# Half a pass less in the first layers, and one chunk of the second MLP ahead of the last chunk of the first

## The chip, the cores and the metric

One core of one Trainium2 chip. The metric is the device time of one execution in microseconds (us). The engines are named as the profile names them: PE (TensorE) with PEld for its weight loads, DVE (VectorE), ACT (ScalarE), POOL (GpSimd), and SP (SyncE), whose queue issues every DMA of this kernel.

## The reference

An RWKV-like recurrence over 768 steps, then two MLPs, each over 3072 tokens of width 320 with a hidden width of 2048:

```python
y_t = r_t @ state                                   # 4 x 8 heads, head_dim 40
state = state * w_t - (state @ a_t) b_t^T + v_t k_t^T
x = y as [3072 tokens, 320]
h = x @ w_in;  x = (h * cos(h)) @ w_out             # first MLP
h = x @ w_in2; out = (s * relu(h)**2 + b) @ w_out2  # second MLP
```

The four weight matrices arrive as 64-bit floats.

## The kernel before

The sequence is cut into 12 chunks c of 64 steps; with 4 batches a chunk is 256 tokens. For each chunk there is a preparation (`prep`: decays, inverse of a triangular matrix), a serial recurrence (`chain`, twice, for the two halves pg of the heads), and the first MLP on the chunk (`mlp` with `m1_f` and `m1_s`). After all of that stands the second MLP, again by 12 chunks j (`m2_f`, `m2_s`). Everything is emitted through `Recorder`, a planner: it collects the instructions of one block (`do` makes a block), gives each a duration and a priority (its longest path to the end, raised by `base`), and writes out an order for each engine by simulating the engines. `schedule(until=...)` does this in three calls: until the preparation's memory is free, until the recurrence's memory is free, to the end. Each engine then works strictly in that order, SP too, so a DMA that waits holds up all DMAs behind it.

Precision: a float32 operand is split in two float16 halves, high and low, and a product takes the passes high x high, high x low and low x high. In `first` a hidden block of 128 columns (ff, 16 of them) takes 8 matmuls of 256 token columns into one PSUM tile `hp`: the 320 input rows stand as 3 heads of 40 on 120 partitions, three groups, of which the last one has only two heads, so that its three products fit in two passes once the low weights have been copied below the high ones (tile `wlo`, two DMAs for each pair of blocks in `w_in_pair`). Two blocks ff = 2p and 2p + 1 share one `hp`; as soon as both are done ACT and DVE (in the first MLP also POOL) make the activation and split it in `gh` and `gl`, and two steps later `m1_s` or `m2_s` does the second layer, 6 matmuls of 320 columns for each half m of the tokens and each p. At most 2 `hp` and 2 `op` (results of the second layer) live at a time; all PSUM tiles come from 8 buffers.

Weights: a raw 64-bit chunk is loaded (`w_in_load`, `w_out_load`), DVE turns it into float32 with three instructions (`float32`), ACT makes the high half, POOL scales in place and makes the low half. For the first MLP raw chunks lie in the memory of the finished weights as far as `place` allows, the others in buffers of tag `xs`. The second MLP's output weights `v2` are loaded when the preparation's memory is free, its input weights `w2` only when the recurrence's memory is free. The recurrence's result goes to DRAM (`xs`, the DMA x<-yhl) and comes back as the MLP's operand (`x1_load`, the DMA xs<-x); the first MLP's result goes through DRAM too (`x2`, the DMA x2f<-x).

All recorded instructions carry line 407, the planner's `emit`, so tiles tell them apart. In the profile w and v stand for both MLPs' weights (numbers are left out of names), wraw and vraw for raw chunks in buffers, XX for the decays, rhp, uhp, ytp, tsp and the like for the recurrence's PSUM tiles.

Of the kernel before, what the change touches and what calls it, by code (L numbers as in the profile page):

```python
# [25 lines left out]
C = 64  # L26
# [3 lines left out]
HEADS = [0, 3, 6, 1, 4, 7, 2, 5]  # L30
# [416 lines left out]
class Fast:  # L447
# [73 lines left out]
    def norm(self, rows, sq, i, k=0):  # L521

        nc = self.nc
        ps = self.pp.tile([128, 2], F32, tag="at", bufs=8, name="np")
        for j, x in enumerate(sq):
            nc.tensor.matmul(ps, x, rows[0:x.shape[0]], start=(j == 0), stop=(j == len(sq) - 1))
        nc.vector.tensor_reduce(out=self.norms[:, k, i:i + 1], in_=ps, axis=AX.X, op=ALU.max)
# [11 lines left out]
    @staticmethod  # L539
    def place(dst, k):  # L540

        q = k + 3 if k < 5 else k if k < 8 else k - 2 if k < 10 else None
        if q is not None:
            return dst[:, 2 * q:2 * q + 2].rearrange("p f a n -> p (f a n)").bitcast(U64)

    def w_in_load(self, src, dst, k):
        p, tag, raws, n = self.wtags[:4]
        raw = self.place(dst, k) if n == 128 else None
        if raw is not None:
            raw = raw.rearrange("p (a n) -> p a n", a=3)  # L550
        else:
            raw = p.tile([120, 3, n], U64, tag=tag, bufs=raws, name="wraw")
        self.RAW["i", k] = raw
        self.nc.sync.dma_start(out=raw, in_=src[:, :, k * n:k * n + n])

    def w_out_load(self, src, dst, k):
        p, tag, raws, n = self.wtags[:4]
        raw = self.place(dst, k) if n == 128 else None
        if raw is None:
            raw = p.tile([128, DM], U64, tag=tag, bufs=raws, name="vraw")  # L560
        self.RAW["o", k] = raw
        self.nc.sync.dma_start(out=raw, in_=src[k * 128:k * 128 + 128, :])

    def w_in_pair(self, dst, name, k):

        nc = self.nc
        p, _, _, n, tag, bufs = self.wtags
        lo = p.tile([80, 2, 128], F16, tag=tag, bufs=bufs, name="wlo")
        m = n // 128
        for i in range(0, 2, m):  # L570
            self.w_in_chunk(dst, name, k * 2 // m + i, n, lo[:, i:i + m])
        for j in range(2):
            nc.sync.dma_start(out=dst[80:120, 2 * k:2 * k + 2, 4 + j], in_=lo[j * 40:j * 40 + 40])

    def w_in_chunk(self, dst, name, k, n, lo):
        nc = self.nc
        raw = self.RAW["i", k]
        st = self.float32(raw)
        m = n // 128
        wv = dst[:, k * m:k * m + m].rearrange("p f a n -> p a f n")  # L580
        sv = st.rearrange("p a (f n) -> p a f n", f=m)
        for a, r, x in ((0, 120, sv[:, 0:2]), (4, 80, bc(sv[0:80, 2], 1, [80, 2, m, 128]))):
            nc.scalar.activation(wv[0:r, a:a + 2], x, AF.Copy, scale=SW)
        nc.gpsimd.tensor_scalar(out=st, in0=st, scalar1=SW, scalar2=1.0, op0=ALU.mult, op1=ALU.mult)
        nc.gpsimd.tensor_tensor(out=wv[:, 2:4], in0=sv[:, 0:2], in1=wv[:, 0:2], op=ALU.subtract)
        nc.gpsimd.tensor_tensor(out=lo, in0=sv[0:80, 2], in1=wv[0:80, 4], op=ALU.subtract)

    def w_out_chunk(self, dst, name, k):
        nc = self.nc
        st = self.float32(self.RAW["o", k])  # L590
# [7 lines left out]
    def w_in_test(self, src, name, k):  # L598

        nc = self.nc  # L600
        sq = self.pm.tile([120, 2, 3, 128], BF16, tag="xs", name="wsq", bufs=4)
        for i, (rows, a, n) in enumerate(((120, 0, 2), (80, 4, 1))):
            nc.scalar.activation(sq[0:rows, :, 2 * i:2 * i + n], src[0:rows, 2 * k:2 * k + 2, a:a + n], AF.Square, scale=1.0 / SW,
                                 accum_out=self.st[0:rows, STAT_IX[name], 2 * k + i:2 * k + i + 1])
        if name == "w1":
            for f in range(2):
                self.norm(self.ones, [sq[0:j, f, i] for i, j in enumerate((120, 120, 80))], 2 * k + f, 1)

    def w_out_test(self, src, name, k):
        self.square(src[:, 2 * k:2 * k + 2, 0], name, k, 1.0 / SW)  # L610
# [821 lines left out]
```

## Time and profile before

| | us |
|---|---|
| median of 3 runs | 1165.01 |
| lowest and highest run | 1154.4, 1169.88 |
| time of the profiled execution | 1152.13 |
| its span, first to last instruction | 1150.4 |
| PE busy in the span | 993.0 (86%) |
| DVE, ACT, POOL busy | 706.4, 728.9, 431.4 |
| mean granted TensorE clock, as a share of full | 0.939 |

The span is the time between the first and the last instruction; the time of that execution has 1.7 us more around it. The profiled execution is shorter than all three timed ones. Busy time of PE counts matmuls by their modelled ends, which overlap, so pauses of a tenth of a microsecond between two matmuls don't show as idle; starts of matmuls do show them.

### The profile page before, as it was taken

To read this page: it belongs to the slowest core of one execution; us is meant where nothing else is said; L and a number is where in the kernel's file an instruction comes from. 1 tells how busy PE (TensorE), PEld (TensorE's weight loads), DVE (VectorE), ACT (ScalarE), POOL (GpSimd) and SP (SyncE) were. 2 spreads that over 40 slices of the span, in tenths; PEclk is the share of its full clock that TensorE was granted. 3 is DMA by queue.
4 is the path that set the end of the run, shared out by engine and by line. 5 is a ranking of instruction groups with operands and counts; after the bars stand their busy time and mean duration, and the time that the engine had idled before them with its cause. 6 is when DMAs were issued, how large, how long until landed. Compare 5 with 4: busy or idle time off the path is not lost.

```text
span 1150.4 us, 37826 instructions
## 1 busy us (share of the span) xinstructions
PE 993.0 (86%) x16094; PEld 802.2 (70%) x16094; DVE 706.4 (61%) x1390; ACT 728.9 (63%) x1608; POOL 431.4 (37%) x430
## 2 busy tenths in 40 slices
PE   3026889998899799979999998938999999999997
PEld 3025667877677687768788786826888888888885
DVE  6799797829563648382848363978454455544443
ACT  3345678968788777767879664735565544544443
POOL 2576649445544454555465422547300000000000
PEclk9998669998899699989999998969999999999999
DMA  9763454444433543443444304473100100001000
GB/s 226 210 201 120 120 190 153 136 139 132 158 103 94 177 139 102 141 152 115 145 152 144 106 30 137 135 185 88 30 24 24 24 24 23 24 24 25 24 15 23
DMA packets 74755, 121.15 MB, mean 105 GB/s; under 512 B 16500, under 2 KB 47348, under 8 KB 73556
## 3 DMA queue, kind: packets, MB, share of 16 engines
q1 hardware_dynamic: 74580, 118.67, 34.1%
q8 instruction: 128, 2.10, 0.7%
q14 instruction: 47, 0.39, 0.1%
HBM read 72.71 MB, written 12.29 MB: 74 GB/s over the span
## 4 chain that ended last, share of the span: by engine, by line
PE 66%; DVE 11%; DMA 8%; SPq 6%; ACT 6%; issue 3%; POOL 0%; ACTq 0%; DVEq 0%
PE hp L407 26%; PE op L407 23%; SPq L407 6%; PE rhp L407 3%; PE ytp L407 3%; PE uhp L407 3%; DVE XX L407 2%; DMA XX<-in_w 2%; DVE wraw L407 2%; DVE v L407 2%; PE dtp L407 1%; DMA x2f<-x 1%; DMA xs<-x 1%; DMA wraw<-in_w 1%; PE ydp L407 1%
## 5 line engine op out<-in xcount | busy, mean ns | idle before, releaser
L407 PEld LDWEIGHTS <-w 120*128 120x128 f16 x3072 | 297.2, 99 | 73.4 <-DMA xs<-x 21.6
L407 PE MATMUL op<-v,gh 128*128 128x320 f16 x1536 | 325.0, 302 | 1.7 <-ACT gh L407 1.7
L407 PE MATMUL op<-v,gl 128*128 128x320 f16 x768 | 231.3, 301 | 1.7 <-POOL gl L407 1.7
L407 PE MATMUL hp<-xs,w 120*128 120x256 f16 x1536 | 204.5, 284 | 23.2 <-DMA xs<-x 22.6
L407 PE MATMUL hp<-x2s,w 120*128 120x256 f16 x1536 | 188.8, 272 | 0.0
L407 POOL TENSOR_TENSOR gl<-q,gh 128x512 f16<-128x512 f32 x96 | 116.5, 1221 | 183.2 <-ACT gh L407 175.8
L407 PEld LDWEIGHTS <-gh 128*128 128x128 f16 x1536 | 143.2, 98 | 49.8 <-ACT gh L407 2.1
L407 DVE SCALAR_TENSOR_TENSOR q<-q,s_t 128x512 f32<-128x512 f32 x96 | 72.3, 753 | 120.8 <-ACT q L407 118.5
L407 ACT ACTIVATE q<-hp 128x512 f32<-128x512 f32 x96 | 57.2, 596 | 126.2 <-PE hp L407 125.9
L407 DVE SCALAR_TENSOR_TENSOR q<-hp,q 128x512 f32<-128x512 f32 x96 | 65.4, 684 | 58.9 <-ACT q L407 58.1
L407 PEld LDWEIGHTS <-gl 128*128 128x128 f16 x768 | 75.4, 98 | 33.0 <-POOL gl L407 2.3
L407 DVE SCALAR_TENSOR_TENSOR gl<-q,b_t,gh 128x512 f16<-128x512 f32 x96 | 72.0, 750 | 38.0 <-ACT gh L407 35.6
L407 ACT ACTIVATE gh<-q,b_t 128x512 f16<-128x512 f32 x96 | 69.1, 720 | 32.3 <-DVE q L407 31.2
L407 ACT ACTIVATE q<-hp,half_pi 128x512 f32<-128x512 f32 x96 | 64.7, 682 | 30.5 <-PE hp L407 29.1
L407 POOL TENSOR_TENSOR kb<-kb,XX 128x512 f32<-128x512 f32 x44 | 57.4, 1316 | 69.8 <-DVE XX L407 47.0
L407 DVE TENSOR_TENSOR_SCAN XX<-XX,starts 128x264 f32<-128x264 f32 x96 | 67.0, 752 | 16.5 <-DMA XX<-in_w 14.2
L407 ACT ACTIVATE gh<-q 128x512 f16<-128x512 f32 x96 | 59.4, 625 | 12.8 <-DVE q L407 12.0
L407 PEld LDWEIGHTS <-KB 120*128 120x128 f16 (+1 forms) x704 | 28.3, 101 | 46.9 <-DMA KB<-kbl 31.4
L407 PE MATMUL rhp<-UF,M 64*64 64x40 f32 (+1 forms) x1536 | 54.2, 230 | 1.0 <-ACT UF L407 0.6
L407 ACT ACTIVATE UF<-uhp 32x320 f32<-32x320 f32 x96 | 41.1, 428 | 22.1 <-PE uhp L407 20.3
L407 ACT ACTIVATE R<-rhp 32x320 f32<-32x320 f32 x96 | 41.1, 429 | 21.4 <-PE rhp L407 19.6
L407 POOL TENSOR_TENSOR kbl<-kb,kbh 128x1024 f16<-128x1024 f32 x22 | 46.8, 2129 | 20.3 <-ACT kbh L407 20.2
(178 smaller groups left out, 1739.3 us busy)
## 6 DMA issues: line engine op xcount, KB each, us to landing
XX<-in_w SPq DMA_DIRECT2D x12, 1056.0 KB
kb<-in_kb SPq DMA_DIRECT2D x24, 512.0 KB
ar<-in_ar SPq DMA_DIRECT2D x22, 512.0 KB
KB<-kbh SPq DMA_DIRECT2D x88, 80.0 KB
ars<-arh SPq DMA_DIRECT2D x88, 80.0 KB
v<-in_v SPq DMA_DIRECT2D x20, 320.0 KB
wraw<-in_w SPq DMA_DIRECT2D x8, 720.0 KB
SS<-SHL SPq DMA_DIRECT2D x88, 50.0 KB
```

Source lines behind the costliest of these rows:

```text
L407: f(*a, **k)
```

## The change

The input rows now stand as 128 + 128 + 64 partitions. `first` does 7 matmuls over all partitions for each hidden block: of the last 64 input rows, high weights and low weights stand one above the other on 128 partitions and multiply the high half of the input in one pass. What is left, high weights by the low half of the last 64 input rows, is a matmul of 64 partitions (`tail`). `rows` puts the tails of a step's two blocks on the partitions 0 to 63, those of the next step's on 64 to 127; `tails` (blocks `m1_t`, `m2_t`) emits the tail of block 2p - 1 and that of block 2p next to each other, ahead of the 7 matmuls of block 2p. The tails of blocks 0 and 15 stand alone. So an `hp` tile is finished one step later, the activation is a block of its own (`m1_g`, `m2_g`) behind that, and 3 `hp` may live at a time. The copies of low weights by DMA (`wlo`) are gone, `x1_load` is 4 DMAs instead of 1.

Of the second MLP's weights, 12 of 16 blocks of both matrices now go into the preparation's memory, with raw chunks in place or in the 5 buffers of tag `xs`; the other 4 go into the recurrence's memory. The first 6 steps of the second MLP's chunk 0 are emitted ahead of the first MLP's last chunk, its rest behind it.

```diff
+    def place(dst, k, size):
+        v = dst.rearrange("p f a n -> p (f a n)")
+        n, part = v.shape[1], v.shape[1] // dst.shape[1]
+        ends = [n - i * size * 4 for i in range(n // (size * 4))]
+        last = dict.fromkeys(ends, -9)
+        for i in range(k + 1):
+            l = [(last[e], e) for e in ends if (e - size * 4) // part > i]
+            q = min(l, default=(i, None))
+            if q[0] >= i - 1:
+                q = (i, None)
+            else:
+                last[q[1]] = i
+        e = q[1]
+        return None if e is None else v[:, e - size * 4:e].bitcast(U64)
...
+    @staticmethod
+    def rows(ff):
+        return ff // 2 % 2 * 64
...
-        for a, r, x in ((0, 120, sv[:, 0:2]), (4, 80, bc(sv[0:80, 2], 1, [80, 2, m, 128]))):
-            nc.scalar.activation(wv[0:r, a:a + 2], x, AF.Copy, scale=SW)
+        nc.scalar.activation(wv[:, 0:3], sv, AF.Copy, scale=SW)
         nc.gpsimd.tensor_scalar(out=st, in0=st, scalar1=SW, scalar2=1.0, op0=ALU.mult, op1=ALU.mult)
-        nc.gpsimd.tensor_tensor(out=wv[:, 2:4], in0=sv[:, 0:2], in1=wv[:, 0:2], op=ALU.subtract)
-        nc.gpsimd.tensor_tensor(out=lo, in0=sv[0:80, 2], in1=wv[0:80, 4], op=ALU.subtract)
+        nc.gpsimd.tensor_tensor(out=wv[:, 3:5], in0=sv[:, 0:2], in1=wv[:, 0:2], op=ALU.subtract)
+        r = slice(64 - self.rows(k * m), 128 - self.rows(k * m))
+        nc.gpsimd.tensor_tensor(out=wv[r, 2], in0=sv[r, 2], in1=wv[r, 2], op=ALU.subtract)
...
+    def second(self, wd, vd, ff0):
+        self.ff0 = ff0
+        for k in range(wd.shape[1]):
+            self.do(self.w_in_load, self.i["w2"], wd, k)
+            self.do(self.w_in_chunk, wd, "w2", k)
+            self.do(self.w_out_load, self.i["v2"], vd, k)
+            self.do(self.w_out_chunk, vd, "v2", k)
...
-        x = self.XS[c] = self.pm.tile([120, 2, 6, 128], F16, tag="xs", name="xs", bufs=4)
-        self.nc.sync.dma_start(out=x, in_=self.x0[c].rearrange("f j p n -> (j p) f n"))
-    def first(self, ps, w, x, ff):
-        for i, (a, b) in enumerate(((0, 0), (0, 1), (1, 2), (1, 3), (2, 0), (3, 2), (4, 4), (5, 5))):
-            self.nc.tensor.matmul(ps, w[:, ff, a], x[:, b // 2, b % 2], start=(ff % 2 == 0 and i == 0), stop=True,
-                                  skip_group_check=True)
+        x = self.XS[c] = self.pm.tile([128, 2, 3, 2, 128], F16, tag="xs", name="xs", bufs=5)
+        v, x = self.x0[c].rearrange("f h e n -> f (h e) n"), x.rearrange("p f i k t -> p f i (k t)")
+        for f in range(2):
+            self.nc.sync.dma_start(out=x[:, f, 0:2], in_=v[f, 0:256].rearrange("(i p) n -> p i n", i=2))
+        for h in range(2):
+            self.nc.sync.dma_start(out=x[h * 64:h * 64 + 64, :, 2], in_=v[:, 256:320].rearrange("f p n -> p f n"))
+    def tail(self, ps, w, x, ff):
+        r = slice(self.rows(ff), self.rows(ff) + 64)
+        self.nc.tensor.matmul(ps[:, ff % 2], w[ff][r, 2], x[r, 2, 1], start=(ff % 2 == 0), stop=True, skip_group_check=True)
+    def tails(self, p, w, x):
+        hp = self.HP
+        hp[p] = self.ph.tile([128, 2, TB], F32, tag="at", bufs=8, name="hp")
+        if p:
+            self.tail(hp[p - 1], w, x, 2 * p - 1)
+        self.tail(hp[p], w, x, 2 * p)
+    def first(self, p, k, w, x):
+        ff, hp = 2 * p + k, self.HP
+        for a, i, b in ((0, 0, 0), (0, 0, 1), (1, 1, 0), (1, 1, 1), (2, 2, 0), (3, 0, 0), (4, 1, 0)):
+            self.nc.tensor.matmul(hp[p][:, k], w[ff][:, a], x[:, i, b], start=False, stop=True, skip_group_check=True)
+        if ff == NFF - 1:
+            self.tail(hp[p], w, x, ff)
...
     def m1_f(self, c, p, k):
-        nc = self.nc
-        if k == 0:
-            self.HP[p] = self.ph.tile([128, 2, TB], F32, tag="at", bufs=8, name="hp")
-        ps, x = self.HP[p], self.XS[c]
-        ff = 2 * p + k
-        self.first(ps[:, k, :], self.w1, x.rearrange("p f (i k) t -> p i k f t", k=2), ff)
-        if k == 0:
-            return
+        x = self.XS[c]
+        self.first(p, k, self.W1, x.rearrange("p f i k t -> p i k f t"))
+    def m1_g(self, c, p):
+        nc, ps = self.nc, self.HP[p]
...
-    def mlp(self, f, s, j):
+    def mlp(self, t, f, g, s, j, lo=0, hi=NFF // 2 + 2):
         lag = 2
-        for p in range(NFF // 2 + lag):
+        for p in range(lo, hi):
             for k in range(2):
                 if p < NFF // 2:
+                    if k == 0:
+                        self.do(t, j, p)
                     self.do(f, j, p, k)
+                if k == 0 and 1 <= p <= NFF // 2:
+                    self.do(g, j, p - 1)
                 if p >= lag:
                     self.do(s, j, p - lag, k)
...
-            rec = self.nc = Recorder(nc, {"any": {"at", "xs", "q"}, "cls": {"XT": 3, "rhp": 3, "hp": 2, "op": 2, "xs": 2, "M2": 2, "q": 4, "att": 6}})
+            rec = self.nc = Recorder(nc, {"any": {"at", "xs", "q"}, "cls": {"XT": 3, "rhp": 3, "hp": 3, "op": 2, "xs": 2, "M2": 2, "q": 4, "att": 6}})
...
-                self.mlp(self.m1_f, self.m1_s, c)
+                if c < NC - 1:
+                    self.mlp(*m1, c)
+                else:
+                    self.nc.base[self.nc.blk] = 26
...
-            self.v2 = pv.tile([128, NFF, 2, DM], F16, name="v2")
-            self.wtags = pv, "vraw", 4, 128, None, 0
-            for k in range(NFF):
-                self.do(self.w_out_load, self.i["v2"], self.v2, k)
-                self.do(self.w_out_chunk, self.v2, "v2", k)
+            n = 12
+            v2 = pv.tile([128, n, 2, DM], F16, name="v2")
+            w2 = pv.tile([128, n, 5, 128], F16, name="w2")
+            self.second(w2, v2, 0)
+            self.W2, self.V2 = ([t[:, f] for f in range(n)] for t in (w2, v2))
+            self.do(self.x2, 0)
+            self.mlp(*m2, 0, 0, n // 2)
+            half = dict(self.HP), dict(self.GH)
+            self.mlp(*m1, NC - 1)
+            self.HP, self.GH = half
             rec.schedule(until=("attn",))
             es_a.close()
             es_b = ExitStack()
             self.pb = pool(es_b, "late")
-            self.w2 = self.pb.tile([120, NFF, 6, 128], F16, name="w2")
-            self.wtags = self.pb, "braw", 6, 256, "blo", 5
-            for k in range(FF // 256):
-                self.do(self.w_in_load, self.i["w2"], self.w2, k)
-                self.do(self.w_in_pair, self.w2, "w2", k)
+            v2b = self.pb.tile([128, NFF - n, 2, DM], F16, name="v2b")
+            w2b = self.pb.tile([128, NFF - n, 5, 128], F16, name="w2b")
+            self.wtags = self.pb, "braw", 8, 128
+            self.second(w2b, v2b, n)
+            self.W2 += [w2b[:, f] for f in range(NFF - n)]
+            self.V2 += [v2b[:, f] for f in range(NFF - n)]
             for j in range(NC):
-                self.do(self.x2, j)
-                self.mlp(self.m2_f, self.m2_s, j)
+                if j:
+                    self.do(self.x2, j)
+                self.mlp(*m2, j, 0 if j else n // 2)
```

## Rows read from the trace of the kernel before

**Rows 1.** The page, parts 1 and 2: busy time, and 40 equal slices.

```profile
PE 993.0 (86%) x16094; PEld 802.2 (70%) x16094; DVE 706.4 (61%) x1390; ACT 728.9 (63%) x1608; POOL 431.4 (37%) x430
...
PE   3026889998899799979999998938999999999997
```

**Rows 2.** Windows: stretch, length; PE, PEld, DVE, ACT, POOL busy; clock; DMA share, GB/s.

```profile
150.00:752.00 602.00, 563.28 (x11694) 453.73 (x11689) 379.13 (x867) 461.24 (x1028) 298.75 (x239) 0.94 0.40 130
752.00:771.00 19.00, 0.16 (x2) 0.00 (x0) 11.17 (x20) 5.06 (x12) 7.25 (x8) 0.62 0.83 203
771.00:805.00 34.00, 28.54 (x213) 21.95 (x214) 29.23 (x30) 18.15 (x35) 26.78 (x22) 0.86 0.44 111
805.00:1141.00 336.00, 336.00 (x2846) 272.23 (x2844) 160.53 (x235) 171.03 (x355) 9.10 (x32) 1.00 0.09 23
```

**Rows 3.** Timeline of PE at 771: start, length, instruction, idle before and releaser.

```profile
771.26 1.03 PE L407 MATMUL hp<-xs,w 120*128 120x256 f16 x4 [19.10 <-DMA xs<-x]
```

**Rows 4.** Timeline of SP, 749 to 762.

```profile
749.95 0.69 SPq L407 DMA_DIRECT2D x<-yhl  x2
754.02 3.63 SPq L407 DMA_DIRECT2D wraw<-in_w  x4
757.69 0.60 SPq L407 DMA_DIRECT2D xs<-x  x1
758.34 3.11 SPq L407 DMA_DIRECT2D wraw<-in_w  x2
```

**Rows 5.** The chain of waits in the second MLP: start, length, piece.

```profile
856.58 2.62 PE hp L407 x24
...
884.30 2.62 PE hp L407 x24
```

**Rows 6.** Timeline of PE around 656, from whole-array matmuls to 40-row transposes.

```profile
655.73 0.30 PE L407 MATMUL op<-v,gh 128*128 128x320 f16 x1
655.86 0.30 PE L407 MATMUL op<-v,gl 128*128 128x320 f16 x1
656.09 0.29 PE L407 MATMUL tsp<-ident,SHL 40*80 40x40 f16 x6
```

**Rows 7.** Timeline of PE, the last of these transposes and what follows it.

```profile
656.38 0.19 PE L407 MATMUL tsp<-ident,SHL 40*80 40x40 f16 x1
656.51 0.31 PE L407 MATMUL op<-v,gh 128*128 128x320 f16 x1
```

**Rows 8.** Timeline of PE at 103.4: two matmuls of 40 rows on different array halves.

```profile
103.40 0.28 PE L407 MATMUL s2p<-ars,XT 40*128 40x64 f32 x2
```

**Rows 9.** Groups by line and form: busy, mean ns of one, idle before, releaser.

```profile
L407 PE MATMUL hp<-xs,w 120*128 120x256 f16 x1536 | 204.5, 284 | 23.2 <-DMA xs<-x 22.6 <-issue 0.5 <-ACT SD L407 0.2
...
L407 DVE SCALAR_TENSOR_TENSOR q<-q,s_t 128x512 f32<-128x512 f32 x96 | 72.3, 753 | 120.8 <-ACT q L407 118.5
L407 DVE SCALAR_TENSOR_TENSOR gl<-q,b_t,gh 128x512 f16<-128x512 f32 x96 | 72.0, 750 | 38.0 <-ACT gh L407 35.6
L407 ACT ACTIVATE gh<-q,b_t 128x512 f16<-128x512 f32 x96 | 69.1, 720 | 32.3 <-DVE q L407 31.2
...
L407 ACT ACTIVATE q<-hp 128x512 f32<-128x512 f32 x96 | 57.2, 596 | 126.2 <-PE hp L407 125.9
```

**Rows 10.** Windows from the release of the preparation's memory on.

```profile
695.00:725.00 30.00, 25.56 (x489) 20.01 (x478) 11.99 (x29) 16.36 (x38) 4.63 (x6) 0.83 0.61 197
725.00:757.00 32.00, 26.71 (x351) 20.75 (x348) 28.84 (x52) 21.78 (x47) 19.13 (x22) 0.99 0.25 75
```

**Rows 11.** Groups by line and form: DVE's conversion of raw chunks.

```profile
L407 DVE SCALAR_TENSOR_TENSOR v<-v 128x320 int32<-128x320 int32 x40 | 31.9, 803 | 0.1
...
L407 DVE SCALAR_TENSOR_TENSOR w<-w 120x384 int32<-120x384 int32 x20 | 18.0, 917 | 0.1
...
L407 DVE TENSOR_SCALAR v<-v 128x320 int32<-128x320 int32 x20 | 10.0, 502 | 11.1 <-DMA v<-in_v 6.5 <-PE np L407 4.6
...
L407 DVE TENSOR_SCALAR w<-w 120x384 int32<-120x384 int32 x10 | 7.2, 718 | 1.0 <-DMA w<-in_w 1.0
```

More of the change, by code (lines that the diff above doesn't have):

```diff
@@ L519, in square, with norm @@
         self.nc.scalar.activation(j, x, AF.Square, scale=scale, accum_out=self.st[rows, STAT_IX[name], i:i + 1])
-    def norm(self, rows, sq, i, k=0):
+    def norm(self, sq, i, k=0):
         nc = self.nc
         ps = self.pp.tile([128, 2], F32, tag="at", bufs=8, name="np")
-        for j, x in enumerate(sq):
-            nc.tensor.matmul(ps, x, rows[0:x.shape[0]], start=(j == 0), stop=(j == len(sq) - 1))
+        for j, (x, rows) in enumerate(sq):
+            nc.tensor.matmul(ps, x, rows, start=(j == 0), stop=(j == len(sq) - 1))
         nc.vector.tensor_reduce(out=self.norms[:, k, i:i + 1], in_=ps, axis=AX.X, op=ALU.max)
@@ L551, in w_in_load @@
         else:
-            raw = p.tile([120, 3, n], U64, tag=tag, bufs=raws, name="wraw")
-        self.RAW["i", k] = raw
-        self.nc.sync.dma_start(out=raw, in_=src[:, :, k * n:k * n + n])
+            raw = p.tile([128, 3, n], U64, tag=tag, bufs=raws, name="wraw")
+        self.RAW["i", dst.tensor.name, k] = raw
+        self.nc.sync.dma_start(out=raw, in_=src[:, :, self.ff0 * 128 + k * n:self.ff0 * 128 + k * n + n])
     def w_out_load(self, src, dst, k):
-        p, tag, raws, n = self.wtags[:4]
@@ L558, in w_out_load @@
-        raw = self.place(dst, k) if n == 128 else None
+        p, tag, raws, n = self.wtags
+        raw = self.place(dst, k, DM) if p is self.pm else None
         if raw is None:
             raw = p.tile([128, DM], U64, tag=tag, bufs=raws, name="vraw")
-        self.RAW["o", k] = raw
-        self.nc.sync.dma_start(out=raw, in_=src[k * 128:k * 128 + 128, :])
-    def w_in_pair(self, dst, name, k):
-        nc = self.nc
[L567 to L573, printed above, removed]
@@ L1006, in yt @@
                              accum_out=self.st[:, STAT_IX["y"], 2 * c + pg:2 * c + pg + 1])
-        self.norm(self.halves, [sq[:, h] for h in range(4)], 2 * c + pg)
+        self.norm([(sq[:, h], self.halves) for h in range(4)], 2 * c + pg)
     def xs(self, c):
@@ new lines, in x2 @@
+        nc.sync.dma_start(out=xt[:, :, 320:384], in_=v[:, :, 256:320])
+        q = self.pm.tile([128, 2, 2, 384], F16, tag="xs", name="x2q", bufs=5)
+        xs = self.XS[NC + j] = self.pm.tile([128, 3, 2, 2, 128], F16, tag="xs", name="x2s", bufs=5)
+        for m in range(2):
+            nc.scalar.activation(q[:, 0, m], xt[:, m], AF.Copy, scale=SX2)
+            nc.vector.scalar_tensor_tensor(out=q[:, 1, m], in0=xt[:, m], scalar=SX2, in1=q[:, 0, m], op0=ALU.mult, op1=ALU.subtract)
+            ps = self.pp.tile([128, 3, 2, 128], F16, tag="at", bufs=8, name="xtp")
+            for i in range(3):
+                for b in range(2):
+                    nc.tensor.transpose(ps[:, i, b], q[:, b, m, i * 128:i * 128 + 128], self.ident)
+            nc.vector.tensor_copy(xs[:, :, :, m], ps)
@@ L1090, in m2_f, with m2_t, m2_g @@
+    def m2_t(self, j, p):
+        x = self.XS[NC + j]
+        self.tails(p, self.W2, x.rearrange("p i b m t -> p i b (m t)"))
+    def m2_f(self, j, p, k):
+        x = self.XS[NC + j]
+        self.first(p, k, self.W2, x.rearrange("p i b m t -> p i b (m t)"))
+    def m2_g(self, j, p):
+        nc, ps = self.nc, self.HP[p]
         q = self.pm.tile([128, 2, TB], F32, tag="q", name="q", bufs=8)
@@ L1233, in run @@
             rec.vector.tensor_copy(self.YT[:, :, 16:32], bc(self.up[:, 0:16], 1, [128, 16, 16]))
-            self.wtags = self.pm, "xs", 4, 128, "wlo", 2
+            self.wtags = self.pm, "xs", 5, 128
+            self.ff0 = 0
+            self.W1, self.V1 = ([t[:, f] for f in range(NFF)] for t in (self.w1, self.v1))
+            m1 = self.m1_t, self.m1_f, self.m1_g, self.m1_s
+            m2 = self.m2_t, self.m2_f, self.m2_g, self.m2_s
             self.prep(0)
```

118 lines of the change are left out of this document (52 added, 66 removed).

## The prediction

> **What bounds the kernel now.** I read the page first: PE is busy in 86% of the span, and its slices show three stages with one hole, the slice that reads 3 between the eights and nines [rows 1]. Then one table of windows cut at those places [rows 2]. From 150 to 752 (recurrence and first MLP) PE is busy 563 of 602 us at a granted clock of 0.94, which is mostly the 2.4 GHz level: almost full, so work taken from or given to PE there counts for most of its price, not all. From 752 to 771 PE stands still. From 771 to 805 it does the last chunk of the first MLP, partly at 1.2 GHz (mean 0.86). From 805 to 1141 it is busy 336 of 336 us at 1.00: the second MLP is bound by PE alone, and what a pass costs there is paid in full. What ends the 19.1 us of idleness is the DMA xs<-x, the operand of the last chunk [rows 3]; SP's timeline says why it is late: four raw weight chunks of 0.72 MB were issued ahead of it as soon as the recurrence's memory was free, and it lands 13.6 us after its issue at 757.69 [rows 4].
>
> **The first layers.** In the second MLP 24 first-layer matmuls stand in the chain with 2.62 us, 109 ns each, and the same piece comes back after 884.30 - 856.58 = 27.72 us, one chunk [rows 5]. Before, a step's two blocks take 16 passes; now 14, and two tails of half the rows. If two tails cost one pass, a chunk saves 7 passes (7 pairs; the tails of blocks 0 and 15 stand alone and save none), 0.76 us. Whether they do is what this prediction hangs on, and the trace has the parts.
>
> *Do two halves of the array work at once?* Yes: two matmuls of 40 rows by 128 columns, on row halves 0 and 64, take 0.28 us together where one takes 0.27: they start 7 ns apart [rows 8].
>
> *What does it cost to get there and back?* The kernel already goes from whole-array matmuls to the half-row kind: the second layer's matmuls start 0.13 us apart (320 columns), but the transposes of 40 rows start 0.23 us after the last of them, 0.093 us late in the unrounded starts [rows 6]. Back again: the last transpose (40 columns, 0.017 us at 109 ns for 256) starts at 656.38, the next whole-array matmul at 656.51, 0.122 us later in the unrounded starts, so 0.10 us late [rows 7]. Some 20 other entries and exits of the same transposes gave the same two figures. Neither pause shows as idle time, since matmuls' modelled ends cover it.
>
> So a pair costs 0.093 + 0.007 + 0.109 + 0.10 = 0.309 us in place of two passes, 0.218: 0.091 us more. A lone tail costs 0.093 + 0.109 + 0.10 = 0.302 in place of 0.109: 0.193 more. A chunk: 7 x 0.091 + 2 x 0.193 = 1.02 us **more**. Bounds: without pauses -0.71 (7 x (0.116 - 0.218)); with pauses and the tails one after the other, 1.02 + 7 x 0.109 = 1.8. I take 1.02: both pauses and the overlap are rows of the same array split with float16 or 128 columns; what no row shows is both tails streaming 256 float16 columns at full rate, hence the upper bound.
>
> The Trainium skill has a rule on each side. "TensorE: Matmul & The Clock Gate", Part 3 on packing, lets tiles on different rows run side by side for about 4 ns each, which by itself gives the saving of 0.71 us a chunk. "TensorEngine Tiling (Array Packing)", Key Properties, says that a change of tiling mode, not of tile alone, drains the engine, which takes the saving back; rows 6 and 7 are that case and price it.
>
> In the second MLP and the last chunk of the first, 13 chunks, this is 13 x 1.02 = **+13.3 us**. In the other 11 chunks, where PE is 94% busy, I count 80%: 11 x 1.02 x 0.8 = **+9.0 us** (0 to 11.2).
>
> **Things that ride along, costed at nothing.** The activation starts one step later. In the second MLP its four instructions take 0.596 + 0.753 + 0.720 + 0.750 = 2.82 us [rows 9], and between the tails and the second layer that needs them PE has two half steps, the next tails and a block: 4 x 0.76 to 0.82 + 0.31 + 0.76 = 4.2 us, where it had 5.1. A shortfall of 0.1 us at each of 96 steps would cost 9.6 us. Three more DMAs per chunk for x1_load are 3 x 0.45 to 0.6 = 1.4 to 1.8 us on SP, so the operand lands that much later; PE's waits for it in the other 11 chunks are 22.6 - 19.1 = 3.5 us in all [rows 9], as other chunks' work covers it; without that cover 11 x 1.8 = 20 us. The DMAs of wlo, one ACT instruction per weight chunk and one per half chunk in x2 go; none of them bounds a stage.
>
> **The hole.** From 752.2 to 1141.4 PE had 389.2 us for work of 27.0 (last chunk of the first MLP: 128 x 0.109 + 96 x 0.136) + 12 x 27.72 = 359.7 us: 29.5 us were waste, 19.1 of them the wait and some 7 the slow 34 us behind it. Now 6 steps of the second MLP can run there: 12 blocks x 7 x 0.109 + 0.302 + 5 x 0.309 + 4 steps x 12 x 0.136 = 17.5 us of PE work, against 19.1 us to fill. The operand itself lands no earlier: 4 blocks of both matrices in raw form are again 2.9 MB that can go ahead of it.
>
> The question is whether the weights are ready. The preparation's memory is free at 695, so 62 us are left until 757. In them DVE was busy 40.8 us and POOL 23.8 [rows 10], v2's conversion included. A w chunk costs DVE 0.72 + 2 x 0.92 = 2.55 us, a v chunk 0.50 + 2 x 0.80 = 2.1 [rows 11]. Moved in: 12 w chunks, 30.6 us; moved out: 4 v chunks, 8.4: net 22 us, for 21.2 us of idle DVE, of which 18 lie in the first 30 us, when raw chunks have only begun to land (8.6 MB at some 200 GB/s is 43 us). So DVE will be full until some 5 to 10 us past 757, the last of the 6 steps wait for it, and behind them in the planner's buffer order the last chunk of the first MLP. I put the waste that stays at 9 us: 1.6 of unfilled wait, 4 for late weights, 3.5 for half of the slow stretch (4 blocks to convert there instead of 16 of w2, so fewer waits). The hole gives **-21 us** (29.5 - 9 = 20.5); bounds: -29.5 if nothing is left, and +1 in the second rival.
>
> **Sum.** 1152.1 + 13.3 + 9.0 - 21 = 1153.4 us for the profiled kind of execution. That execution was 12.9 us shorter than the median of the three runs; with that added the forecast is 1166 us, no change. Two per cent are 23 us; less can hardly be told from none in runs that differ by 15 us among themselves. With the ends of the terms that I hold to be open (9.0 from 0 to 11.2, the hole from -29.5 to -5) the forecast's own range is 1148 to 1184.
>
> **Rivals.** *A, no pause* (the packing rule above as written): a pair costs 0.116, a chunk saves 0.71 us, 13 x 0.71 + 11 x 0.71 x 0.8 = 15.5 us, with the hole 36.5: 1128 us. For it: the two halves overlap [rows 8]. Against it: rows 6 and 7, met at every entry. It would need PE to treat 64 rows of matmul otherwise than 40 rows of transpose. 0.17.
>
> *B, slower: the conversions crowd the recurrence out of DVE.* The 22 us of moved conversions stand in DVE's fixed order among the instructions of the recurrence's last chunk, with a priority that v2's did not have, since the second MLP's steps now hang on them. If all of it goes in ahead, the recurrence ends at 771 instead of 749, the operand of the last chunk lands at 793, 17.5 us of filler are used up by 769, and the waste is 41 - 17.5 + 7 = 30.5: nothing is gained. 1152.1 + 13.3 + 9 + 1 + 12.9 = 1188 us. The gain of the hole falls to nothing at a slip of some 20 us; each us less gives one back. For it: DVE at 28.8 of 32 us in 725 to 757 already. Against it: 18 us idle just before, and filler for PE meanwhile. 0.15.
>
> *C, tails one after the other*: 13 x 0.76 + 11 x 0.76 x 0.8 = 17 us more than the forecast, 1183, still within 2% but slower. 0.08.
>
> The forecast has 0.60.
>
> **How the numbers follow.** The range is 1130 to 1190: it takes in the forecast's own range, C, B's price and the half of A nearest to it; left out are the other half of A and what B may cost beyond its price, some 0.15. Faster by over 2% (below 1142): A's 0.17 and 0.04 of the forecast's low end, 0.21. Slower by over 2% (above 1188): half of B, 0.03 of C, and 0.06 for the forecast's high end with a shortfall at the activation, 0.17. Within: 0.62.
>
> **What would show it.** In the second MLP the first-layer pattern comes back after 28.7 us (forecast), 27.0 (A) or 29.5 (C) instead of 27.72, and the starts around a pair of tails show 0.20 us before and 0.21 behind it. At the end of the recurrence PE has no gap over 5 us, and second-MLP matmuls stand before the last chunk of the first; under B there is a gap of 10 us or more that DVE's conversions or xs<-x end. The prediction is wrong in its size if the first 150 us move, which I left alone, or if the planner's order holds back DMAs of the recurrence on SP behind raw loads that wait for their place.

## The result, and the profile after

The changed kernel took 1150.01 us (median of 4 runs, 1145.39 to 1154.19), the kernel before 1166.89 beside it; the ratio is 0.9894, interval 0.9846 to 0.9942. Forecast was no change, 1166: by the ratio, which is used from here on, the kernel became 1.06% or some 12 us faster (the two medians, of four runs each, lie 16.9 us apart). The profiled execution took 1145.39 us, its span is 1143.7, 6.7 us less than before; both profiled executions are at the fast end of their runs.

The page's slices of PE and its clock, and the stages by windows:

```profile
PE   3037698998999999898999998599999999999996
PEclk9998689899989999999999999699999999999999
```

```profile
core 0: us, PE busy (x) PEld busy (x) DVE busy (x) ACT busy (x) POOL busy (x), PEclk, DMA share, GB/s
0.00:50.00 50.00, 12.87 (x129) 11.94 (x129) 39.96 (x95) 17.98 (x44) 20.22 (x58) 1.00 0.86 275
150.00:700.00 550.00, 517.52 (x10983) 401.82 (x10984) 365.37 (x805) 424.62 (x935) 285.30 (x226) 0.97 0.42 135
700.00:752.00 52.00, 35.06 (x490) 25.61 (x489) 49.83 (x83) 28.33 (x59) 37.26 (x46) 0.80 0.51 163
752.00:805.00 53.00, 53.00 (x433) 39.01 (x432) 28.16 (x42) 25.17 (x45) 23.15 (x23) 1.00 0.08 22
805.00:1124.00 319.00, 319.00 (x2624) 235.25 (x2622) 152.94 (x218) 158.64 (x319) 2.10 (x25) 1.00 0.10 25
```

Against [rows 1, 2]: the stretch from 752, where PE stood still for 19 us and then ran slowly, is full (53.00 of 53 at clock 1.00). A shallower hole stands ahead of it, in the slice that reads 5: 35 of 52 us busy, with DVE at 49.8 of 52. What PE waits for there is partly the operand of chunk 10 (in [rows 3] it was that of chunk 11, the last one), partly DVE's and ACT's work at the end of the recurrence:

```profile
engine line waited for: us in total, times, longest us
PE hp L406 <- DMA xs<-x: 7.4, 1, 7.4
PE np L406 <- ACT ysq L406: 5.8, 2, 4.7
PE s2p L406 <- DMA XT<-XT: 1.9, 1, 1.9
```

The chain in the second MLP (start, us, instruction, count), the counterpart of [rows 5], here a step and a half; the `hp` piece of nine matmuls is seven full passes and two tails:

```profile
844.68 1.63 PE op L406 x12
846.31 0.98 PE hp L406 x9
847.29 0.92 PE op L406 x6
848.22 0.76 PE hp L406 x7
848.98 0.81 PE op L406 x6
```

The nine take 0.98 us, what nine full passes take: the pause into the half-row mode has eaten the pass that was saved. The `op` piece behind the tails takes 0.92 us where the next one takes 0.81: the pause on the way back. In the unrounded starts a tail begins 0.205 us after a full pass (0.109 otherwise) or 0.231 after an `op` pass (0.136 otherwise), 0.096 late; two tails start 3 to 4 ns apart; what follows them starts 0.212 us later, 0.10 late. So pauses and overlap are as read from [rows 6 to 8], and the chunk comes back after 871.1 - 842.5 = 28.6 us instead of 27.7 (forecast 28.7).

What nobody forecast stands at the other end of the trace. The first matmul of the first MLP starts at 150.8 us instead of 159.3, the recurrence's chunk 9 is done (DVE's last instruction on its result) at 624.8 instead of 646.2, and the last chunk, 11, at 723.0 instead of 747.9. So something was gained before the reordered part began. How much of this lead is time gained, the experiments have to tell.

### The profile page after: what moved, and what is told of

It is laid out like the page before. It is cut to its first block, busy times and chain, and to the rows that moved or that the text cites. A ratio compares the mean times of both kernels' runs of the same rounds, so it can differ in the third digit from the quotient of the medians.

```text
span 1143.7 us, 37859 instructions
## 1 busy us (share of the span) xinstructions
PE 1005.5 (88%) x16094; PEld 768.7 (67%) x16094; DVE 739.4 (65%) x1414; ACT 717.4 (63%) x1544; POOL 444.0 (39%) x454
## 4 chain that ended last, share of the span: by engine, by line
PE 70%; DVE 8%; DMA 7%; ACT 5%; POOL 4%; issue 3%; SPq 2%; POOLq 0%; ACTq 0%; DVEq 0%
PE hp L406 26%; PE op L406 25%; PE rhp L406 4%; SPq L406 2%; PE ytp L406 2%; PE uhp L406 2%; DVE XX L406 2%; DMA XX<-in_w 2%; DVE v L406 2%; PE txp L406 1%; PE s1p L406 1%; PE spp L406 1%; PE dtp L406 1%; PE opx L406 1%; DMA XT<-XT 1%
## 5 line engine op out<-in xcount | busy, mean ns | idle before, releaser
L406 PEld LDWEIGHTS <-w 128*128 128x128 f16 (+1 forms) x2688 | 240.3, 98 | 86.3 <-issue 34.8
L406 PE MATMUL op<-v,gh 128*128 128x320 f16 x1296 | 274.8, 302 | 0.4 <-ACT gh L406 0.4
L406 PE MATMUL hp<-xs,w 128*128 128x256 f16 (+1 forms) x1536 | 205.5, 279 | 14.3 <-DMA xs<-x 7.4
L406 PE MATMUL op<-v,gl 128*128 128x320 f16 x648 | 195.0, 301 | 1.1 <-POOL gl L406 1.1
L406 PEld LDWEIGHTS <-gh 128*128 128x128 f16 x1536 | 135.7, 98 | 57.2 <-issue 3.7
L406 PE MATMUL hp<-x2s,w 128*128 128x256 f16 (+1 forms) x1152 | 149.6, 274 | 0.0
L406 ACT ACTIVATE gh<-q 128x512 f16<-128x512 f32 x96 | 59.9, 626 | 23.4 <-DVE q L406 22.4
L406 POOL TENSOR_TENSOR arl<-ar,arh 128x1024 f16<-128x1024 f32 x22 | 48.0, 2182 | 28.6 <-ACT arh L406 28.4
L406 POOL TENSOR_TENSOR kbl<-kb,kbh 128x1024 f16<-128x1024 f32 x22 | 47.8, 2173 | 28.6 <-ACT kbh L406 27.4
L406 ACT ACTIVATE XT<-txp 80x1024 f16<-80x1024 f16 (+1 forms) x52 | 48.0, 948 | 11.6 <-PE txp L406 11.2
```

The costliest lines, as they stand in the source:

```text
L406: f(*a, **k)
```

## The experiments

Ratios are to the kernel before on the same chip, with their 95% intervals; 1% is 11.6 us.

**1. full_tails.** Each tail as one pass over the whole array:

```diff
-        r = slice(self.rows(ff), self.rows(ff) + 64)
-        self.nc.tensor.matmul(ps[:, ff % 2], w[ff][r, 2], x[r, 2, 1], ...)
+        self.nc.tensor.matmul(ps[:, ff % 2], w[ff][:, 2], x[:, 2, 1], ...)
```

> The changed kernel with each tail as one matmul over all 128 rows (it then also adds the low-by-low products of the last 64 inputs, terms that neither kernel computes): a chunk has 8 full passes a block again, but no switch between whole-array and half-array matmuls. If the switch is what the tails cost (0.096 us in and 0.10 out in the trace of the changed kernel), a full tail starts 3 to 110 ns after its neighbour with no pause, the second MLP's chunk period falls from 28.61 us to about 27.7, its last eleven and a half chunks give back about 10.5 us, the first MLP 5 to 8 more, and the time is about 1133 us. If the period of 28.61 us has another cause (the activation one step later, the new operand layout), it stays at 28.5 or rises by the eight tails that no longer overlap, and the time is 1150 us or more.

1139.59 us, ratio 0.9849 (0.9798 to 0.99), some 6 us above the expected 1133. The second MLP's period falls to 27.7 and it gives back 10.2 us, but the first MLP starts at 157.4 instead of 150.8, since the planner, told of longer tails, wrote another order (with the order held it is 150.4, experiment 7). Half the question is answered; the other half needs the order held (experiment 7).

**2. chunk0_behind.**

```diff
-            self.do(self.x2, 0)
-            self.mlp(*m2, 0, 0, n // 2)
...
             self.mlp(*m1, NC - 1)
...
-                self.mlp(*m2, j, 0 if j else n // 2)
+                self.do(self.x2, j)
+                self.mlp(*m2, j)
```

> The changed kernel with all of the second MLP's chunk 0 put behind the last chunk of the first MLP, as in the kernel before; the memory of the weights, and so their early loads and conversions, stay as changed. If the reorder fills the hole at the end of the recurrence, as the prediction had it, a gap of about 15 to 19 us that ends with the operand of the last chunk comes back between 750 and 772, the second MLP starts after 800 instead of at 753, and the time is 8 to 20 us above the changed kernel's 1150, about 1164. Rival: the gain comes from the first 150 us and from the earlier conversions; the reorder itself is worth nothing, the time stays within 4 us of 1150.

1167.79 us, ratio 1.0111 (1.0059 to 1.0163): 2.2% or 25 us above the changed kernel. The reorder does fill the hole. From 700 to 805, where the changed kernel leaves PE idle for 16.9 us, this one leaves 30.7. The long gap that came back stands not at 750 to 772, as expected, but ends at 745.47, after 20.0 us:

```profile
700.00:752.00 52.00, 25.31 (x412) 18.68 (x410) 51.48 (x79) 24.28 (x53) 37.94 (x51) 0.70 0.50 155
752.00:805.00 53.00, 48.99 (x397) 35.52 (x395) 23.24 (x40) 23.69 (x44) 23.75 (x23) 0.97 0.10 30
...
745.47 11.44 PE L406 MATMUL hp<-xs,w 64*128 64x256 f16 x79 [19.97 <-DMA xs<-x]
```

What PE waits for is the operand of chunk 10, and SP's timeline says why it is late. Chunk 10's result goes out at 709.16. Its operand is issued at 735.24, behind chunk 11's result and eight raw weight chunks:

```profile
709.16 0.74 SPq L406 DMA_DIRECT2D x<-yhl  x2
...
726.24 0.74 SPq L406 DMA_DIRECT2D x<-yhl  x2
729.99 0.56 SPq L406 DMA_DIRECT2D wraw<-in_w  x1
...
734.34 0.79 SPq L406 DMA_DIRECT2D vraw<-in_v  x1
735.24 2.77 SPq L406 DMA_DIRECT2D xs<-x  x4
```

**3. passes_alone.** The other half of the change by itself:

```diff
-            n = 12
-            v2 = pv.tile([128, n, 2, DM], F16, name="v2")
-            w2 = pv.tile([128, n, 5, 128], F16, name="w2")
+            v2 = pv.tile([128, NFF, 2, DM], F16, name="v2")
...
+            w2 = self.pb.tile([128, NFF, 5, 128], F16, name="w2")
```

> Only the first part of the change: layout on 128 rows and 7.5 passes; the second MLP's weights lie and arrive as in the kernel before (all of v2 in the preparation's memory, all of w2 in the recurrence's) and nothing is reordered. The prediction's terms give +13.3 and +9.0 us, about 1188 on a median of 1165.9 to 1167. With the first MLP starting 8 us earlier, as in the changed kernel, it would be 1176 to 1180. Rival: the layout's early start outweighs the switches and the first part is neutral or better, 1160 to 1167, so that the second part is worth only some 10 us.

1159.55 us, ratio 1.0026 (0.9994 to 1.0058): nearer the rival than the prediction's terms. The first MLP starts at 150.0, yet the kernel is no faster than the one before. The second part is worth the difference to 0.9894, 1.3% or 15 us. Since chunk0_behind is 0.85% above this kernel, the second part is two things: the weights moved into the preparation's memory, with the order that the planner then writes, cost 10 us, and the reorder brings 25.

What the 10 us are is argued, not shown. DVE converts the second MLP's weights for 21 us between 650 and 706 (2.2 here), and the recurrence's chunk 10 ends at 705.0 in the changed kernel and at 706.1 in chunk0_behind, though chunk 9 is done at 625 to 627; here it is 641.6 and 693.8. But the recurrence as a whole is not late there: its last chunk ends at 723.0 and 723.9, and here at 744.6. What is lost is PE's work meanwhile: from 700 to 810 PE is idle for 30.7 us in chunk0_behind and for 22.1 here, where chunk 10's operand is issued from 702.95 on.

**4. loads_128.** The kernel before, its raw loads on 128 partitions; eight rows are repeated in the input and read by no matmul:

```diff
-            raw = p.tile([120, 3, n], U64, tag=tag, bufs=raws, name="wraw")
+            raw = p.tile([128, 3, n], U64, tag=tag, bufs=raws, name="wraw")
...
-            self.nc.tensor.matmul(ps, w[:, ff, a], ...)
+            self.nc.tensor.matmul(ps, w[0:120, ff, a], ...)
```

> The kernel before with one thing changed: the raw chunks of the first layers' weights arrive on 128 partitions instead of 120 (eight rows are repeated as padding and read by no matmul). In the changed kernel the first MLP starts at 150.8 us instead of 159.3, with 0.6 us instead of 0.9 us on SP for each such load. If the 128-partition load is the cause, the first MLP starts at about 151 to 154 here too, and the time falls by some 4 to 8 us. If the cause is that the small low-part DMAs are gone, or the planner's other order of the first loads, it starts at 158 to 160 and the time is as before.

1132.68 us, ratio 0.9804 (0.9757 to 0.9851): a gain of 23 us, three times what was expected, and 10 us better than the whole change. The first MLP starts at 147.6, the recurrence ends at 731.5 instead of 747.9.

**5 and 6. The loads, or the order that the planner makes for them?** The planner prices a DMA by its partitions (`0.45 if full else 0.75`), so loads_128 also has another order on every engine. Two kernels separate them. In each the planner is told the other price: rows128_old_order has the loads on 128 partitions in the order of the kernel before, rows120_new_order has those on 120 in the order of loads_128. In the traces every engine's order is that of its counterpart.

```diff
+        w = (out.dtype == U64 and out.space == SBUF and len(out.ap) == 3)
...
-        full = ... == 128
+        full = ... == 128 and not w        # rows128_old_order; "or w" in rows120_new_order
```

> Loads of raw weights on 128 partitions, as in loads_128 (which took 1132.68 us, ratio 0.9804), but the planner is told that they cost what 120 partitions cost, so that every engine issues its instructions in exactly the order of the kernel before. If the loads themselves are faster (in the traces a DMA packet of 1024 bytes takes 54 ns in loads_128 and 79 ns in the kernel before, its issue on SP 0.6 and 0.87 us), the time falls to 1133 to 1143 with no change of order, and the first MLP starts at 148 to 153 us. If the gain is the planner's other order, the time stays at 1155 to 1167 and the first MLP starts at 157 to 160.

1148.19 us, ratio 0.9876 (0.9842 to 0.991). The first MLP starts at 156.5, not at the expected 148 to 153, and the time lies between the two that were expected.

> The other corner: the kernel before with its loads on 120 partitions, but the planner told that they cost what 128 cost, so that every engine issues in exactly the order of loads_128. If the loads are the cause, 1155 to 1170 (the order is made for loads that land sooner, so it may wait more). If the order is the cause, about 1133.

1147.43 us, ratio 0.9866 (0.9822 to 0.991). Neither theory has it all: the loads alone bring 1.2%, the order alone 1.3%, both together 2.0%. What the loads do is seen where the order is the same. SP's queue in the kernel before and in rows128_old_order:

```profile
12.88 1.96 SPq L407 DMA_DIRECT2D w<-in_w  x2
16.14 2.70 SPq L407 DMA_DIRECT2D w<-in_w  x3
```

```profile
13.20 1.33 SPq L407 DMA_DIRECT2D w<-in_w  x2
15.88 1.92 SPq L407 DMA_DIRECT2D w<-in_w  x3
```

and their windows (before first):

```profile
12.00:28.00 16.00, 9.59 (x94) 9.37 (x94) 15.66 (x32) 7.00 (x22) 3.42 (x6) 1.00 1.14 237
28.00:42.00 14.00, 2.71 (x40) 2.48 (x38) 7.92 (x24) 6.36 (x17) 5.95 (x11) 1.00 1.06 315
42.00:50.00 8.00, 0.00 (x0) 0.00 (x0) 8.00 (x18) 1.92 (x5) 3.69 (x4) 1.00 0.92 214
```

```profile
12.00:28.00 16.00, 9.23 (x86) 9.01 (x88) 15.86 (x32) 6.70 (x21) 3.41 (x6) 1.00 1.14 316
28.00:42.00 14.00, 3.06 (x47) 2.83 (x44) 13.97 (x27) 8.47 (x23) 9.70 (x14) 1.00 0.99 348
42.00:50.00 8.00, 0.00 (x0) 0.00 (x0) 8.00 (x19) 0.00 (x0) 3.87 (x4) 1.00 0.14 40
```

An issue takes 0.65 us instead of 0.9 to 1.0. More than that, the DMA engines are full (share 1.14) in both from 12 to 28, and move 237 GB/s in one and 316 in the other; the raw v chunks of this stretch have landed by 43.5 instead of 50.2. DVE, which in the kernel before stands half idle from 28 to 42 (7.92 of 14 us) because v<-in_v has not landed, is busy 13.97. The inverse of chunk 0 that is queued behind those conversions starts earlier, and chunk 0 of the recurrence is done at 134.2 instead of 139.8.

This lead does not last. Chunk 2 is done at 255.4 instead of 252.7, chunk 11 at 746.3 instead of 747.9. The rest of what the two spans differ by (1150.4 and 1144.6) is won in the hole, where the raw chunks that stand ahead of the last operand in SP's queue are now quicker too:

```profile
748.33 0.70 SPq L407 DMA_DIRECT2D x<-yhl  x2
752.41 2.85 SPq L407 DMA_DIRECT2D wraw<-in_w  x4
755.30 0.85 SPq L407 DMA_DIRECT2D xs<-x  x1
...
768.09 2.31 PE L407 MATMUL hp<-xs,w 120*128 120x256 f16 x10 [17.55 <-DMA xs<-x]
```

From the issue of x<-yhl to the first matmul on the operand it takes 19.8 us here, 21.3 in [rows 3, 4], and the second MLP starts at 798.4 instead of 803.9. In the other pair of equal order, rows120_new_order and loads_128, the recurrence's end moves from 737.9 to 731.5 and this way from 30.7 to 23.4. So the faster loads pay at both ends. How the 14 us of rows128_old_order divide is open, since the two profiled executions differ by 5.8 us only.

**7. full_tails_same_order.** full_tails, with the planner told of half tails:

```diff
+        self.nc.plan = [w[ff][r, 2], x[r, 2, 1]]
         self.nc.tensor.matmul(ps[:, ff % 2], w[ff][:, 2], x[:, 2, 1], ...)
```

> The changed kernel with tails over all 128 rows, as in full_tails (1139.59 us, ratio 0.9849), but the planner counts each tail with half its rows, so that every engine issues in exactly the order of the changed kernel; only the switch between array modes goes, and some tails of the first chunk read low parts not yet subtracted. The first MLP starts at 150 to 152 us again. By the prediction's prices the time falls by 10.7 us in the second MLP and by 5 to 9 in the first, against the changed kernel's ratio of 0.9894: 0.975 to 0.980, some 1131 to 1137 us. If the switch costs nothing in the first MLP, because PE waits there anyway, only the second MLP's 10 us come back, 0.980 to 0.982.

1135.16 us, ratio 0.9762 (0.9729 to 0.9795): the mode switch costs the changed kernel 1.3% or 15 us, as expected; the two profiled spans differ by 10.6, of which eleven chunks of the second MLP give 10.2. In the chain the pause behind the tails is gone (0.82 instead of 0.92), and nine full passes take the same 0.98:

```profile
845.09 0.98 PE hp L406 x9
846.07 0.82 PE op L406 x6
846.88 0.76 PE hp L406 x7
847.65 0.81 PE op L406 x6
```

**8. full_tails_ten.**

```diff
-        e = q[1]
+        e = q[1] if k < 10 else None
```

> full_tails with one thing of the kernel before put back: only the first ten raw chunks of each weight matrix of the first MLP may be loaded into the memory of converted weights, the rest wait for one of the five buffers, so fewer conversions stand on DVE ahead of the first chunk of the recurrence. In the trace of full_tails DVE is busy from 70 to 140 us without a pause, 21 instructions on v among them (9 in loads_128), and the first MLP starts at 157.4 us against 147.6 in loads_128. If these early conversions are what delays it, it starts at 148 to 152 here and the time is 1128 to 1135; if not, 1137 to 1145.

1145.59 us, ratio 0.9839 (0.9801 to 0.9878), no better than full_tails. The first MLP does start at 153.7 instead of 157.4, but its chunk 3 starts at 332.1 instead of 318.2; that the raw chunks that wait hold it up is likely and not shown. The theory got part of the start right and the time wrong.

**9. loads_alone.** Loads without a computation:

```diff
+        for n in (128, 120, 124, 112, 96, 64, 128, 120, 112):
+            t = [p.tile([128, 3, 128], U64, tag=f"raw{k}", bufs=1, name=f"r{n}_") for k in range(8)]
+            for k in range(8):
+                nc.sync.dma_start(out=t[k][0:n], in_=ins["w1"][0:n, :, k * 128:k * 128 + 128])
+            for k in range(8):
+                nc.vector.tensor_copy(d[0:n, k:k + 1], t[k].bitcast(I32)[0:n, 0, 0:1])
```

> Only the loads, nothing of the computation (the output is zeros): nine batches of eight raw weight loads of three runs of 1024 bytes per partition, on 128, 120, 124, 112, 96, 64, 128, 120 and 112 partitions, each batch behind the one before. If a load on 120 partitions is slower by itself, its batch (2.95 MB) takes longer than that on 128 (3.15 MB): by the packets of the two kernels (79 and 54 ns) some 11 to 12 us against 8 to 9. If what matters is a number of partitions that 16 divides, 112 is as fast per byte as 128, and 124 as slow as 120; if it is 128 alone, 112 and 96 are slow too. If the loads are equal by themselves, all batches move the same GB/s and the difference comes from what runs beside them.

DVE copies one element of each tile as soon as it lands, so its starts show when loads land. Two each of the batches on 120, 124, 128 and 112 partitions:

```profile
19.67 0.15 DVE L1424 COPY d<-r__87 120x1 int32<-120x1 int32 x1 [1.39 <-DMA r__87<-in_w]
21.22 0.15 DVE L1424 COPY d<-r__88 120x1 int32<-120x1 int32 x1 [1.39 <-DMA r__88<-in_w]
...
34.73 0.15 DVE L1424 COPY d<-r__110 124x1 int32<-124x1 int32 x1 [3.89 <-DMA r__110<-in_w]
38.78 0.15 DVE L1424 COPY d<-r__111 124x1 int32<-124x1 int32 x1 [3.89 <-DMA r__111<-in_w]
...
94.82 0.15 DVE L1424 COPY d<-r__206 128x1 int32<-128x1 int32 x1 [0.98 <-DMA r__206<-in_w]
95.95 0.15 DVE L1424 COPY d<-r__207 128x1 int32<-128x1 int32 x1 [0.98 <-DMA r__207<-in_w]
...
123.83 0.15 DVE L1424 COPY d<-r__258 112x1 int32<-112x1 int32 x1 [0.76 <-DMA r__258<-in_w]
124.73 0.15 DVE L1424 COPY d<-r__259 112x1 int32<-112x1 int32 x1 [0.75 <-DMA r__259<-in_w]
```

The starts are 1.55 us apart on 120 partitions, and 1.65 in the second batch. On 128 they are 1.13 apart, with more data, for four loads of the second batch, until the loads on 120 behind them run too (then 1.55 to 1.72). On 124 they are 4.05 apart. So the load on 120 is slower by itself than the one on 128, and that on 124 by far the slowest, which no expectation had. For 112 the run does not settle it: 1.5 in the first batch, 1.3 and at the end 0.90 in the second; 96 and 64 came out at 1.5 and 0.9. The batches overlap their neighbours, and this is one run.

**10 and 11. rows128_reorder, rows128_reorder6.** loads_128 with the second part of the change, as far as six matrices a block leave room:

```diff
+            n = 8                          # 6 in rows128_reorder6
+            v2 = pv.tile([128, n, 2, DM], F16, name="v2")
+            w2 = pv.tile([128, n, 6, 128], F16, name="w2")
+            self.second(w2, v2, 0)
...
+            self.mlp(*m2, 0, 0, n // 2)
             self.mlp(*m1, NC - 1)
```

(The priority of the last operand is 13 instead of 26 in the first and 26 in the second; the second has 4 operand buffers, the first 5.)

> loads_128 (ratio 0.9804: eight full passes a block on 120 rows, no switch of array modes) with the second part of the change on top: 8 of the second MLP's 16 blocks of both matrices in the preparation's memory (with six matrices a block, 12 do not fit), and four steps of its chunk 0 ahead of the first MLP's last chunk. If the parts add, as their prices in the other runs do (the second part was worth 1.3% on top of passes_alone), a third less for the fewer blocks: ratio 0.968 to 0.974, about 1130 us or less on a chip whose before is 1163. If the faster loads have already shortened the hole (the operand of the last chunk waits for 0.5 us a DMA less), the second part is worth nothing here: 0.978 to 0.985.

1136.93 us, ratio 0.9771 (0.9726 to 0.9816): against the 0.9804 of loads_128 nothing that can be told.

> The same with 6 blocks instead of 8, three steps ahead, and one operand buffer fewer: less filler for the hole (8.5 us of matmuls instead of 11.5), fewer conversions beside the end of the recurrence. If the filler decides, 2 to 4 us more than rows128_reorder; if the crowding of DVE decides, less than it.

1125.4 us, ratio 0.9648 (0.9599 to 0.9697), the fastest of all: less moved is better, as the crowding of DVE would have it, but buffers, priority and with them the whole order differ too, so this is not shown. From 700 to 805 PE is busy for 96.6 of 105 us:

```profile
700.00:752.00 52.00, 49.92 (x696) 40.26 (x694) 35.35 (x63) 33.70 (x75) 28.66 (x32) 1.00 0.48 142
752.00:805.00 53.00, 46.70 (x373) 36.19 (x371) 51.50 (x75) 29.17 (x67) 32.63 (x41) 0.97 0.33 99
```

**12. order_nudge.**

```diff
-        return 0.45 if full else 0.75, ...
+        return 0.45 if full else 0.80, ...
```

> The kernel before with one constant of its planner moved: a DMA on fewer than 128 partitions is planned with 0.80 us of issue instead of 0.75 (the trace has 0.87). No instruction changes, only the order in which each engine issues them. rows120_new_order showed 1.3% for an order alone. If that order was good because it was planned for cheaper loads, this one is 0 to 0.5% slower than the kernel before or the same. If any other order of the same work moves the time by a per cent either way, the ratio is off 1 by 0.5 to 1.5% in one direction or the other.

1165.0 us, ratio 1.0033 (0.9995 to 1.0071): an order made for dearer loads is no better, although its first MLP starts at 155.8 instead of 159.3 and its recurrence has chunk 0 done at 134.6 instead of 139.8; its last chunk is done at 756.3, 8 us late. One nudge is no distribution, but the 1.3% of rows120_new_order is not what any new order brings.

**13. layout_alone.** passes_alone with the edit of experiment 7.

> passes_alone (ratio 1.0026) with each tail over all 128 rows, planned as a half so that every engine issues in exactly the order of passes_alone; some tails of the first chunk read low parts not yet subtracted. What is left of the change is its layout on 128 rows in five matrices a block, with four operand DMAs a chunk. Against loads_128 (0.9804) passes_alone lost 2.2%, 26 us. If the switch of array modes is all of that loss, this kernel comes back to 0.980. If the switch costs here the 1.3% that it cost in the changed kernel, the ratio is 0.989 and the other 11 us belong to the layout and its order.

1141.9 us, ratio 0.9832 (0.9794 to 0.9871). The switch costs this pair 1.9% or 22.6 us (17 between the two profiled spans, 10 of them in the second MLP); the layout with its order is within 0.3% of loads_128, as expected if the switch is all of the loss.

## Why the prediction was wrong, point by point

**The step that failed is the one that costed things at nothing.** "Things that ride along, costed at nothing" and "the first 150 us ... which I left alone" pass over an edit that is in the change: the raw loads go from 120 to 128 partitions, by the same two lines as in experiment 4. Alone it is worth 2.0% or 23 us (loads_128), and the new layout without its mode switch is worth 1.7% or 20 us (layout_alone). It pays in two ways that overlap: DMAs that are faster by themselves (1.2% at the same order) and an order planned for them (1.3% by itself). PE's idleness in the first 150 us is in [rows 1] (its first slices read 3, 0, 2, 6); it was taken for a fixed prologue, and not asked what ends it. The same loads stand in [rows 4] ahead of the last operand, and there too their length was taken as given. The kernel's own planner had a higher price for a DMA on fewer than 128 partitions.

**The first layers** were priced rightly where a pass is paid in full. In the second MLP a chunk lost 0.89 us of the forecast 1.02; the planner set one of the two lone tails of each chunk beside a pair, so that three tails share one switch (in the trace 8 switches a chunk instead of 9). Over the whole kernel the forecast was +22.3 us. It is 22.6 between passes_alone and layout_alone (17.2 between their spans), but 15 in the changed kernel (10.6 between the spans), where PE in the profiled executions starts the second MLP's chunk 1 at 813.9 with the switch and at 813.8 without: there the 9.0 us of the first MLP did not show. The mean granted clock from 150 to 700 is 0.97 with the switch and 0.95 without. Rivals A (no pause) and C (tails in turn) are refuted by the starts of the tails. "TensorEngine Tiling (Array Packing)" of the Trainium skill, Key Properties, was the rule that held.

**The activation one step later and the three more operand DMAs** cost nothing that can be told: without the switch the new layout, which has both, is as fast as loads_128 within the intervals (0.9832 and 0.9804, each known to some 0.4 or 0.5%). They were not measured each by itself.

**The hole** gave 15 us instead of 21, as the difference of two larger things: the reorder brought 25, and moving the weights took 10 back. Rival B had foreseen a loss, but not this one. It had the recurrence end at 771 instead of 749; it ended 25 us earlier than before (723.0). What came late is chunk 10 (705.0 instead of 693.7, while chunk 9 was 21 us ahead). The likely reason, not shown by itself, is that the preparation's memory came free at 670 instead of 695, so that the moved conversions met that chunk and not the last one; its operand came late too. PE's gap of 7.4 us there is one that the forecast's "no gap over 5 us" excluded: the chunk's result went out at 707.9, its operand was issued from 724.4 on. The prediction's last sentence had named a move of the first 150 us and DMAs held back on SP as ways to be wrong in size, and priced neither.

**Together**, in the prediction's own terms: -20 (the layout without its switch, forecast 0) + 23 (the switch, forecast +22) - 15 (the second part, forecast -21) = -12 us, the measured change. These terms add up by construction, since each kernel is one step from the next; by another way the switch is 15. That 1150 lies inside the range of 1130 to 1190 is no merit of the sum: the missing term was about as large as each of the other two.

The Trainium skill had the rule that was missed. "DMA: Bandwidth & Descriptors", section "Why a DMA increments its semaphore by 16 and not by 1", says that a DMA takes the largest number of engines, up to 16, that divides the outermost dimension of both its sides. For these loads that is 16 for 112 and 128 partitions, 15 for 120 and 4 for 124. The run agrees for 124: 4.05 us a load, and from 31 to 55 us a DMA share of 0.30. For 120 it would explain one engine of 16, where the load took 1.55 us against 1.13; what the rest is remains open.

## What to carry to other kernels

Ask of every edit, padding too, what it does to each DMA's partition count, and look for all places where such a DMA ends a wait: here ahead of the first chunk and again ahead of the last operand. An earlier start is not yet a gain: order_nudge had chunk 0 done 5 us earlier and ended no sooner, and in rows128_old_order 1.6 us of a lead of 5.6 were left at the last chunk. Where a planner writes the order, hold its prices fixed to see what an edit does by itself; an edit and the new order can each be worth more than the effect looked for. A half-array pass that saves time on paper must stand in a long enough run to pay for two mode switches of 0.1 us; by the starts measured here two pairs in a row would about break even (an estimate: 0.20 + 4 x 0.109 / 2 = 0.42 us against 0.44 for four full passes).

## What the runs showed of the hardware

Each load of three runs of 1024 bytes per partition took 4.05 us on 124 partitions, 1.55 to 1.65 on 120 and 1.13 on 128 where no loads on 120 ran beside it (loads_alone, one run). In the first 60 us of the traces a packet of 1024 bytes takes 79 ns in the kernel before and 54 in rows128_old_order, and the packets of 2560 bytes beside it, whose loads are unchanged, go from 132 to 113.

A matmul on 64 rows behind one on all 128 starts 0.096 us late, the next one on 128 rows 0.10 us late; two on different halves of the rows start 3 to 4 ns apart (after).
